# Second half of the first weight slab issued by another engine, narrower dummies, and a split last store in a two-layer SiLU kernel

## The chip, the cores and the metric

The kernel runs on one core of a Trainium2 chip. A core has five engines, each with its own instruction stream: TensorE (PE, matrix multiplications into PSUM), VectorE (DVE), ScalarE (ACT), GpSimd (POOL) and SyncE (SP). They wait for one another through semaphores. Data comes from and goes to the device memory by DMA: SyncE and ScalarE issue a transfer, which then runs by itself on 16 shared DMA engines and raises a semaphore when it has landed. The metric is the device time of one execution in microseconds (us), taken as the median of several runs.

## The reference

```python
# x: (1, 2048, 640), w1: (640, 1728), w2: (1728, 640), all bf16
h = jnp.einsum("bsd,df->bsf", x, w1)
h = jax.nn.silu(h)
out = jnp.einsum("bsf,fd->bsd", h, w2)
```

## The kernel before

The first layer is computed with the hidden dimension on the partitions: `hT` holds 13 tiles of 128 hidden columns, and a tail of 64 in `hTt`. The inner dimension of 640 is cut into five pieces k = 0 to 4 of 128. The 2048 rows of x are taken in four pieces c of 512. x must be there with its inner dimension on the partitions (`xT`), so it is loaded by transposing DMAs (`turned`, L119), three for each piece c: k = 0 and 1, k = 2 and 3, k = 4. The weights `w1s` of the first eight hidden tiles come as five slabs, one for each k (`load_k`, L125; 256 KB each); slab 0 comes in two halves of four hidden tiles (128 KB each). The other hidden columns follow in two loads (L165 to 169).

For the first piece c = 0 the order is by slabs: `k_pass(k)` (L201) runs eight matmuls, one for each hidden tile, into eight PSUM banks, and the five passes k add up there. Pass k = 0 needs the first x load and the first half of slab 0; ahead of its fifth matmul it waits for the second half (L203 and 204). After that come the remaining five hidden tiles of c = 0, then the pieces c = 1 to 3, then the tail. ScalarE takes each finished bank through Silu into `hT` (L195).

The second layer follows without a break on TensorE: for each of 16 tiles of 128 rows, `finish` (L297) adds 13 matmuls of 512 output columns to what `open_pair` began, and VectorE and ScalarE in turn copy the bank to `o_sb` (`evac`, L252). The last 128 of the 640 output columns are made separately, turned (`oT`), and put into `o_sb` by a transposing DMA before the last ten tiles are computed (L329 to 351). `store` (L310) lets SyncE wait for the evictions of a tile and write it to the output. The last tile is made in two parts, columns 0 to 384 and 384 to 512; the second part is stored together with the last 128 columns, so its store has 256 columns.

Some things stand before the start. The program begins with a preamble that ends in a barrier of all engines. `ahead_of_start` (L98) puts an instruction before an engine's part in this barrier, and `barrier_wait_here` (L109) moves an engine's wait for it to the place where it is called. Ahead of the barrier SyncE issues the first x load, slab 1, the second x load, slab 2 and slab 3 (L156 to 162); ScalarE issues the first half of slab 0. VectorE clears a tile `z`, and TensorE runs 14 dummy matmuls of 256 columns on it (L141 to 148), whose results nobody reads; the fourth one raises a semaphore. ScalarE waits for that (L172), issues the second half of slab 0 (L173), and only then waits for the barrier (L174). TensorE waits for the barrier after pass k = 1 (L214), SyncE after all its weight loads (L170). After the barrier GpSimd clears `warm`, and ScalarE runs one Silu on it, which loads the table of that function (L176 to 178).

Of the kernel before, what the change touches and what calls it, by code (L numbers as in the profile page):

```python
# [9 lines left out]
def bass_standalone__dense_activation_silu__prompt_kernel(  # L10
# [6 lines left out]
    bf16 = mybir.dt.bfloat16  # L17
# [3 lines left out]
    of = out.flatten_outer_dims()  # L21
    S, D = xf.shape
    F = w1.shape[1]
    P = 128
    NB = 8
# [5 lines left out]
    HB = 256  # L31
    NSC = S // SCH
    DA = 512
# [4 lines left out]
    pe, act, dve, pool, sp = nc.tensor, nc.scalar, nc.vector, nc.gpsimd, nc.sync  # L38

    with ExitStack() as es:  # L40
        def sb(name, shape, dtype):
            return es.enter_context(nc.sbuf_tensor(name, shape, dtype))

        xT = sb("xT", [P, DT, S], bf16)
        w1s = sb("w1s", [P, DT, F], bf16)
# [4 lines left out]
        oT = sb("oT", [P, S], bf16)  # L50
        o_sb = sb("o_sb", [P, S // P, D], bf16)
        warm = sb("warm", [P, 32], fp32)
        z = sb("z", [P, HB], bf16)
        ps = es.enter_context(nc.psum_tensor("ps", [P, NB, BANK], fp32))

        count = {}
# [2 lines left out]
        def sem(name):  # L59
            s = es.enter_context(nc.semaphore(name))  # L60
            count[s.name if hasattr(s, "name") else name] = 0
            return [s, 0]

        def tick(ins, s, n=1):
            ins.then_inc(s[0], n)
            s[1] += n
            return (s, s[1])

        def wait(eng, *points):
            for pt in points:  # L70
                if pt is None:
                    continue
                s, v = pt
                key = (id(eng), id(s))
                if seen.get(key, 0) < v:
                    eng.wait_ge(s[0], v)
                    seen[key] = v

        s_pe, s_act, s_dve = sem("s_pe"), sem("s_act"), sem("s_dve")
# [4 lines left out]
        def load(eng, out_ap, in_ap):  # L84
            s = sem(f"s_ld{n_dma[0]}")
            n_dma[0] += 1
            return tick(eng.dma_start(out=out_ap, in_=in_ap), s, 16)

        ET = mybir.EngineType

        def preamble(engine, opcode):
            lst = nc.main_func.blocks[0].instructions
            return next(
                i for i, ins in enumerate(lst)
                if ins.opcode == opcode and ins.engine == engine
            )

        def ahead_of_start(emit, engine):  # L98
            lst = nc.main_func.blocks[0].instructions
            n = len(lst)  # L100
            r = emit()
            lst = nc.main_func.blocks[0].instructions
            new = lst[n:]
            del lst[n:]
            at = preamble(engine, "Drain")
            lst[at:at] = new
            return r

        def barrier_wait_here(engine):  # L109
            lst = nc.main_func.blocks[0].instructions  # L110
            lst.append(lst.pop(preamble(engine, "EventSemaphore")))

        w1_v = w1.rearrange("(dt p) f -> p dt f", p=P)
        w2_v = w2[0:F0, :].rearrange("(ft p) d -> p ft d", p=P)

        FA = 8
# [8 lines left out]
        def load_k(eng, k):  # L125
            return load(eng, w1s[:, k, 0:FA * P], w1_v[:, k, 0:FA * P])
# [6 lines left out]
        def first(i):  # L133
            k0, k1 = KT[i]
            pt = turned(0, k0, k1, s_x[i])
            for k in range(k0, k1):
                ld_x[k] = pt
        p_z = ahead_of_start(lambda: tick(dve.memset(z[:, :], 0.0), s_dve), ET.DVE)  # L138
        bank_free = [None] * NB

        def dummies(n):  # L141
            for _ in range(n):
                ins = pe.matmul(ps[:, 3, 0:HB], lhsT=z[:, 0:P], rhs=z[:, :], start=True, stop=True)  # L143
            return tick(ins, s_pe)

        wait(pe, p_z)
        p_d0 = dummies(4)
        dummies(10)

        FH = FA // 2  # L150
        ld_k = {}

        def slab(k):
            ld_k[k] = load_k(sp, k)

        ahead_of_start(lambda: first(0), ET.SP)  # L156
        ld_k0a = ahead_of_start(
            lambda: load(act, w1s[:, 0, 0:FH * P], w1_v[:, 0, 0:FH * P]), ET.Activation)
        ahead_of_start(lambda: slab(1), ET.SP)
        ahead_of_start(lambda: first(1), ET.SP)  # L160
        ahead_of_start(lambda: slab(2), ET.SP)
# [3 lines left out]
        for a, b in FG:  # L165
            e = F if b == FT else b * P
# [1 line left out]
            for ft in range(a, b):  # L168
                ld_w1[ft] = pt
        barrier_wait_here(ET.SP)  # L170

        wait(act, p_d0)  # L172
        ld_k[0] = load(act, w1s[:, 0, FH * P:FA * P], w1_v[:, 0, FH * P:FA * P])  # L173
        barrier_wait_here(ET.Activation)  # L174

        p_warm = tick(pool.memset(warm[:, :], 0.0), s_pool)  # L176
        wait(act, p_warm)
# [3 lines left out]
        for c in range(1, NSC):  # L181
# [6 lines left out]
            load(sp, w2t[0:FL, :], w2[F0:F, :]),  # L188
            load(sp, w2t[FL:2 * FL, :], w2[F0:F, :]),
        ]  # L190

        def mm(o, l, r, start, stop, shared=False):
            return pe.matmul(o, lhsT=l, rhs=r, start=start, stop=stop, skip_group_check=shared)  # L193
# [30 lines left out]
        for ft in range(FA, FT):  # L224
            wait(pe, ld_w1[ft])
            b = bank()
            for k in range(DT):
                ins = mm(ps[:, b, :], w1s[:, k, ft * P:(ft + 1) * P], xT[:, k, 0:SCH],
                         start=(k == 0), stop=(k == DT - 1))
            silu(hT[:, ft, 0:SCH], ps[:, b, :], b, tick(ins, s_pe))  # L230
        for c in range(1, NSC):
            wait(pe, ld_xc[c])
            for ft in range(FT):
                b = bank()
                for k in range(DT):
                    ins = mm(ps[:, b, :], w1s[:, k, ft * P:(ft + 1) * P],
                             xT[:, k, c * SCH:(c + 1) * SCH], start=(k == 0), stop=(k == DT - 1))
                h_last = silu(hT[:, ft, c * SCH:(c + 1) * SCH], ps[:, b, :], b, tick(ins, s_pe))
        h_tail = []
        for q in range(NSC // 2):  # L240
            b = bank()
            for k in range(DT):
                for hh in range(2):
                    c = 2 * q + hh
                    ins = mm(ps[hh * FL:(hh + 1) * FL, b, :], w1s[:, k, F0:F],
                             xT[:, k, c * SCH:(c + 1) * SCH],
                             start=(k == 0), stop=(k == DT - 1), shared=True)
# [4 lines left out]
        def evac(out_ap, in_ap, b, after, eng=None):  # L252
            e = eng or (dve, act)[evac_n[0] % 2]
            evac_n[0] += 1
            wait(e, after)
            if e is dve:
                r = tick(dve.tensor_copy(out=out_ap, in_=in_ap), s_dve)  # L257
            else:
                r = tick(act.copy(out=out_ap, in_=in_ap), s_act)  # L259
            bank_free[b] = r  # L260
            return r

        st_w = [None] * NSC
# [25 lines left out]
        JB = SCH // P  # L289
# [4 lines left out]
        last_st = order[-1]  # L294
# [13 lines left out]
            return fin  # L308

        def store(st, fin):  # L310
            lo = 0
            for a, e, r in fin:
                hi = D if e == DA else e
                wait(sp, r, st_w[st // JB])
                stores.append(load(sp, of[st * P:(st + 1) * P, lo:hi], o_sb[:, st, lo:hi]))
                lo = hi

        def open_pairs(sts):
            for i in range(0, len(sts), 2):
# [2 lines left out]
        stores = []  # L322
# [7 lines left out]
        for c in range(NSC):  # L330
            b = bank()
            wbank.append(b)
            for ft in range(FT):
                mm(ps[:, b, :], w2s[:, ft, DA:D], hT[:, ft, c * SCH:(c + 1) * SCH],
                   start=(ft == 0), stop=False)
        wait(pe, *h_tail)
        for q in range(NSC // 2):
# [6 lines left out]
            for hh in range(2):  # L344
                c = 2 * q + hh
                r = evac(oT[:, c * SCH:(c + 1) * SCH], ps[:, wbank[c], :], wbank[c], tt[hh])
# [5 lines left out]
        for st, fin in early:  # L352
            store(st, fin)
        for bt in batches[1:]:
            open_pairs(bt)
            for st in bt:
                store(st, finish(st))
# [29 lines left out]
```

## Time and profile before

| what | value |
|---|---|
| median of 5 runs | 125.82 us (125.63 to 125.92) |
| profiled execution, its own time | 125.91 us |
| its span, from first to last instruction | 124.6 us |
| granted TensorE clock in it | 1.00 |
| TensorE busy | 121.1 us (97%), 588 matmuls |
| ScalarE busy | 38.1 us (31%) |
| VectorE busy | 7.5 us (6%) |
| DMA | 10.35 MB in 19285 packets |
| dummies | 14, mean 419 ns |
| first-layer matmuls | 280, mean 381 ns |

The span is shorter than the time, since the time also holds what lies before the first and after the last instruction. A matmul's duration reaches from its start to its modelled end; since matmuls are pipelined, the distance from one start to the next is shorter than the duration, and it is the distance that sets the time of a run of matmuls. A DMA row on SyncE or ScalarE gives the time that the engine spends on issuing; the landing comes later, and has a view of its own that gives the time from the start of the issue to the landing. The idle time printed behind an instruction names what released the engine.

### The profile page before, as it was taken

To read this page: it belongs to the slowest core of one execution; us is meant where nothing else is said; L and a number is where in the kernel's file an instruction comes from. 1 tells how busy PE (TensorE), PEld (TensorE's weight loads), DVE (VectorE), ACT (ScalarE), POOL (GpSimd) and SP (SyncE) were. 2 spreads that over 40 slices of the span, in tenths; PEclk is the share of its full clock that TensorE was granted. 3 is DMA by queue.
4 is the path that set the end of the run, shared out by engine and by line. 5 is a ranking of instruction groups with operands and counts; after the bars stand their busy time and mean duration, and the time that the engine had idled before them with its cause. 6 is when DMAs were issued, how large, how long until landed. Compare 5 with 4: busy or idle time off the path is not lost.

```text
span 124.6 us, 1342 instructions
## 1 busy us (share of the span) xinstructions
PE 121.1 (97%) x588; PEld 55.2 (44%) x588; DVE 7.5 (6%) x12; ACT 38.1 (31%) x66; POOL 0.3 (0%) x5
## 2 busy tenths in 40 slices
PE   8699999999999999999999999999999999999993
PEld 6144444444444444444434444444434444444452
DVE  0000000000000000000002020200012220102021
ACT  0400985555555555555530101010012101010100
POOL 0000000000000000000000000000000000000000
DMA  6999999799000000000000000000003377111112
GB/s 131 206 322 305 177 180 119 134 358 363 0 0 0 0 5 0 3 0 0 0 0 0 5 0 0 0 0 0 0 0 70 62 252 264 53 53 53 53 59 99
DMA packets 19285, 10.35 MB, mean 83 GB/s; under 512 B 13264, under 2 KB 18768, under 8 KB 19280
## 3 DMA queue, kind: packets, MB, share of 16 engines
q1 hardware_dynamic: 18992, 10.01, 31.7%
q10 hardware_dynamic: 288, 0.26, 0.9%
q8 instruction: 4, 0.07, 0.2%
q14 instruction: 1, 0.01, 0.0%
HBM read 4.51 MB, written 2.62 MB: 57 GB/s over the span
## 4 chain that ended last, share of the span: by engine, by line
PE 94%; DMA 4%; issue 0%; ACT 0%; DVEq 0%
PE ps L193 94%; DMA w1s<-in_w_dram 4%; PE ps L143 1%; ACT o_sb L259 0%; DVEq L372 0%
## 5 line engine op out<-in xcount | busy, mean ns | idle before, releaser
L193 PE MATMUL ps<-xT,w1s 128*128 128x512 bf16 (+1 forms) x280 | 59.1, 381 | 1.1 <-DMA w1s<-in_w_dram 1.1
L193 PE MATMUL ps<-w2s,hT 128*128 128x512 bf16 (+2 forms) x221 | 45.4, 367 | 0.0
L193 PEld LDWEIGHTS ps<-xT,w1s 128*128 128x128 bf16 (+1 forms) x280 | 26.4, 99 | 33.7 <-DMA w1s<-in_w_dram 1.6
L197 ACT ACTIVATE hT<-ps 128x512 bf16<-128x512 f32 x52 | 30.0, 608 | 25.8 <-PE ps L193 25.8
L193 PEld LDWEIGHTS ps<-w2s,hT 128*128 128x128 bf16 x221 | 20.9, 98 | 24.4 <-issue 1.1
L259 ACT CAST o_sb<-ps 128x512 bf16<-128x512 f32 (+1 forms) x8 | 4.4, 545 | 42.2 <-PE ps L193 42.2
L257 DVE CAST o_sb<-ps 128x512 bf16<-128x512 f32 (+1 forms) x9 | 6.1, 676 | 101.1 <-PE ps L193 101.1
L193 PE MATMUL ps<-hT,w2s 128*128 128x512 bf16 x52 | 11.4, 379 | 0.0
L193 PEld LDWEIGHTS ps<-hT,w2s 128*128 128x128 bf16 x52 | 5.1, 98 | 6.1
L259 ACT CAST oT<-ps 128x512 bf16<-128x512 f32 x2 | 1.1, 588 | 11.0 <-PE ps L193 11.0
L143 PE MATMUL ps<-z 128*128 128x256 bf16 x14 | 3.2, 419 | 0.4 <-DVE z L138 0.4
L178 ACT ACT_TABLE_LOAD x1 | 1.3, 1283 | 4.8 <-DVEq L372 4.8
L143 PEld LDWEIGHTS ps<-z 128*128 128x128 bf16 x14 | 2.0, 146 | 1.1 <-DVE z L138 0.4
L193 PE MATMUL ps<-w2t,hTt 64*128 64x512 bf16 (+2 forms) x17 | 2.2, 366 | 0.0
L257 DVE CAST oT<-ps 128x512 bf16<-128x512 f32 x2 | 1.3, 686 | 13.7 <-PE ps L193 13.7
L197 ACT ACTIVATE hTt<-ps 128x512 bf16<-128x512 f32 x2 | 1.2, 597 | 1.1 <-PE ps L193 1.1
L193 PEld LDWEIGHTS ps<-w2t,hTt 64*128 64x128 bf16 x17 | 0.7, 94 | 1.4 <-issue 0.8
L193 PE MATMUL ps<-hTt,w2t 64*128 64x512 bf16 x4 | 0.6, 382 | 0.0
L193 PEld LDWEIGHTS ps<-hTt,w2t 64*128 64x128 bf16 x4 | 0.1, 94 | 0.4 <-issue 0.4
L178 ACT ACTIVATE warm<-warm 128x32 f32<-128x32 f32 x1 | 0.2, 229 | 0.0
L138 DVE MEMSET z<- 128x128 uint32 x1 | 0.2, 165 | 0.2 <-issue 0.2
L176 POOL MEMSET warm<- 128x32 f32 x1 | 0.1, 124 | 4.3 <-POOLq L372 4.3
(4 smaller groups left out, 0.4 us busy)
## 6 DMA issues: line engine op xcount, KB each, us to landing
out_dram<-o_sb SPq DMA_DIRECT2D x15, 160.0 KB, 1.9
w2s<-in_w_dram SPq DMA_DIRECT2D x1, 1120.0 KB, 5.7
w1s<-in_w_dram SPq DMA_DIRECT2D x4, 256.0 KB, 4.4
w2s<-in_w_dram SPq DMA_DIRECT2D x1, 960.0 KB, 7.8
w1s<-in_w_dram SPq DMA_DIRECT2D x1, 480.0 KB, 5.1
w1s<-in_w_dram SPq DMA_DIRECT2D x1, 400.0 KB, 5.9
w1s<-in_w_dram ACTq DMA_DIRECT2D x2, 128.0 KB, 3.4
xT<-in_x_dram SPq DMA_TRANSPOSE x12, 4.5
```

What stands on the lines that cost most here:

```text
L138: p_z = ahead_of_start(lambda: tick(dve.memset(z[:, :], 0.0), s_dve), ET.DVE)
L143: ins = pe.matmul(ps[:, 3, 0:HB], lhsT=z[:, 0:P], rhs=z[:, :], start=True, stop=True)
L176: p_warm = tick(pool.memset(warm[:, :], 0.0), s_pool)
L178: act.activation(out=warm[:, :], in_=warm[:, :], func=ACT.Silu)
L193: return pe.matmul(o, lhsT=l, rhs=r, start=start, stop=stop, skip_group_check=shared)
L197: r = tick(act.activation(out=out_ap, in_=in_ap, func=ACT.Silu), s_act)
L257: r = tick(dve.tensor_copy(out=out_ap, in_=in_ap), s_dve)
L259: r = tick(act.copy(out=out_ap, in_=in_ap), s_act)
```

## The change

There are three edits. The second half of slab 0 is issued by SyncE, ahead of the barrier, between the first x load and slab 1; ScalarE's wait for the dummies, its issue and the moved barrier wait are gone, so ScalarE waits for the barrier where the preamble has it. The dummy tile `z` has 128 columns, of which a repeating access pattern reads each twice, so a dummy still streams 256 columns; there are 13, and none raises a semaphore. Their code stands further down in the program, but on TensorE they are still the first instructions. In `store`, the last 128 columns of the last tile are stored on their own, as soon as they are turned, before SyncE waits for the two other parts; the last store has 128 columns.

```diff
-        z = sb("z", [P, HB], bf16)
+        z = sb("z", [P, P], bf16)
...
-        bank_free = [None] * NB
-
-        def dummies(n):
-            for _ in range(n):
-                ins = pe.matmul(ps[:, 3, 0:HB], lhsT=z[:, 0:P], rhs=z[:, :], start=True, stop=True)
-            return tick(ins, s_pe)
-
-        wait(pe, p_z)
-        p_d0 = dummies(4)
-        dummies(10)
-
         FH = FA // 2
         ld_k = {}
...
         ahead_of_start(lambda: first(0), ET.SP)
         ld_k0a = ahead_of_start(
             lambda: load(act, w1s[:, 0, 0:FH * P], w1_v[:, 0, 0:FH * P]), ET.Activation)
+        ld_k[0] = ahead_of_start(
+            lambda: load(sp, w1s[:, 0, FH * P:FA * P], w1_v[:, 0, FH * P:FA * P]), ET.SP)
         ahead_of_start(lambda: slab(1), ET.SP)
         ahead_of_start(lambda: first(1), ET.SP)
         ahead_of_start(lambda: slab(2), ET.SP)
...
         barrier_wait_here(ET.SP)
 
-        wait(act, p_d0)
-        ld_k[0] = load(act, w1s[:, 0, FH * P:FA * P], w1_v[:, 0, FH * P:FA * P])
-        barrier_wait_here(ET.Activation)
-
         p_warm = tick(pool.memset(warm[:, :], 0.0), s_pool)
...
+        bank_free = [None] * NB
+
+        z2 = z[:, :].rearrange("p (o n) -> p o n", o=1).to_broadcast([P, HB // P, P])
+
+        def dummies(n):
+            for _ in range(n):
+                pe.matmul(ps[:, 3, 0:HB], lhsT=z[:, 0:P], rhs=z2, start=True, stop=True)
+
+        wait(pe, p_z)
+        dummies(13)
...
         def store(st, fin):
-            lo = 0
+            def out_cols(a, e):
+                stores.append(load(sp, of[st * P:(st + 1) * P, a:e], o_sb[:, st, a:e]))
+
+            wait(sp, st_w[st // JB])
+            if st == last_st:
+                out_cols(DA, D)
             for a, e, r in fin:
-                hi = D if e == DA else e
-                wait(sp, r, st_w[st // JB])
-                stores.append(load(sp, of[st * P:(st + 1) * P, lo:hi], o_sb[:, st, lo:hi]))
-                lo = hi
+                wait(sp, r)
+                out_cols(a, D if st != last_st else e)
```

## The prediction

> **What bounds the kernel now.** I read the page's busy shares first: TensorE (PE) is busy 97% of a span of 124.6 us, so only what delays the first long run of matmuls, interrupts it, or follows the last one can count. Then the chain of work that ended last, in order of time (start us, length us, what):
>
> ```profile
> 0.39 1.05 PE ps L143 x4
> 1.44 0.02 issue
> 1.46 4.48 DMA w1s<-in_w_dram
> 5.94 0.05 issue
> 5.99 116.67 PE ps L193 x569
> 122.66 0.02 issue
> 122.68 0.27 ACT o_sb L259
> ```
>
> The reader is to see three pieces: a weight load that ScalarE issues at 1.46, after four dummies, and that lands at 5.94; then 569 matmuls without a gap from 5.99 on; then the last eviction, and its store up to 124.6. So whatever moves the start of the unbroken run moves the end one for one, unless a later load is not there in time. The timeline of the first 12 us shows what stands before that start (start us, length us, engine, line, idle before it):
>
> ```profile
> 0.39 3.17 PE L143 MATMUL ps<-z 128*128 128x256 bf16 x14 [0.39 <-DVE z L138]
> ...
> 3.52 1.35 PE L193 MATMUL ps<-xT,w1s 128*128 128x512 bf16 x4
> ...
> 5.99 6.22 PE L193 MATMUL ps<-xT,w1s 128*128 128x512 bf16 x28 [1.12 <-DMA w1s<-in_w_dram]
> ```
>
> Four matmuls of pass k=0 run on the first half of weight slab 0, then TensorE stands still for 1.12 us for the second half. The issue view, taken for a window that holds just these two issues (KB, us from issue to landing), gives the two loads that decide:
>
> ```profile
> w1s<-in_w_dram SPq DMA_DIRECT2D x1, 256.0 KB, 4.8
> w1s<-in_w_dram ACTq DMA_DIRECT2D x1, 128.0 KB, 4.5
> ```
>
> The second half of slab 0 lands at 1.46 + 4.5 = 5.96, slab 1 at 1.39 + 4.8 = 6.2: both are in flight together. Slab 1 isn't waited for now, since its pass begins at 5.99 + 4 x 0.216 = 6.85. SyncE's issues ahead of the barrier:
>
> ```profile
> 0.00 1.33 SPq L120 DMA_TRANSPOSE xT<-in_x_dram  x1
> 1.39 0.56 SPq L87 DMA_DIRECT2D w1s<-in_w_dram  x1
> 2.01 1.24 SPq L120 DMA_TRANSPOSE xT<-in_x_dram  x1
> 3.29 1.05 SPq L87 DMA_DIRECT2D w1s<-in_w_dram  x2
> ```
>
> **Rates.** 28 matmuls in 6.22 us, less the 0.38 that the last one takes, are 0.216 us each (512 columns). Fourteen dummies in 3.17, less 0.42, are 0.2115 each for 256 columns, so 0.423 for 512: half the rate. The first four real ones take (1.35 - 0.38) / 3 = 0.323 from start to start, 0.32 us more than at full rate, so about 1.5 of them ran at half rate: the rate rises near 3.52 + 1.5 x 0.423 = 4.15, which is 3.8 us after the first dummy. The row's granted clock is 1.00 throughout and doesn't show this; the spacing does.
>
> **The change, part by part.**
>
> 1. *Second half of slab 0 from SyncE, behind the first transposed load.* Its issue moves from 1.46 (ScalarE, behind the wait for four dummies) to 1.39, where slab 1's issue stands now. In a queue of its own order it is then behind the first x load, which lands at 3.52, and ahead of slab 1. Bounds for its landing: 1.39 + 2.4 = 3.8 (the first half took 2.4 us) and 1.39 + 4.5 = 5.9 (as now). TensorE is ready for it at 3.52 + 0.97 + 0.216 = 4.71 and done with it, if it is there, at 4.71 + 4 x 0.216 = 5.57. Then it wants slab 1. Any landing up to about 5.5 therefore has the same answer, and I take one in that part of the range.
>
> 2. *What is late next: slab 1.* Every issue behind the moved one on SyncE's queue moves by one issue. ScalarE's rows for this same piece are 0.34 and 0.38 us long, SyncE's for the larger slab 0.56; with the 0.06 between issues that is 0.40 to 0.62; I take 0.42, the row of the same shape. Slab 1's landing: 6.2 if it is set by the bytes that share the DMA engines (the same 384 KB as now, in another order), 6.2 + 0.42 to 6.2 + 0.62 if it rides on its issue. I take half of the shift, 6.4, because both loads start well after issue now and land within 0.3 us of each other, which speaks for sharing, while nothing excludes that the issue counts. Pass k=1 then starts at 6.4 + 0.05 (the issue gap of the chain) = 6.45 in place of 6.85: **0.40 us gained** of the 1.12.
>
> 3. *The later passes.* k=2 starts at 6.45 + 8 x 0.216 = 8.18. With 0.42 added in full, its x load (2.01 + 5.1 = 7.1) comes at 7.5 and slab 2 (3.29 + 4.4 = 7.7) at 8.1: just in time. k=3 at 9.91 has slab 3 at 8.8, k=4 at 11.6 slab 4 at 10.4, the next weight columns 11.9 against 13.4, the last 13.2 against 16.6, and the next 512 rows of x (third load 12.57 + 4.3 = 16.9) 17.3 against 18.8. No new wait, if nothing slips by more than the 0.42; the tightest cover is 0.1 us, at slab 2.
>
> 4. *Barrier.* SyncE reaches it after its early issues, so it also opens some 0.42 later. Behind it stand the POOL memset and ScalarE's table load (4.75, 1.28 us) and warm activation (to 6.28). ScalarE's next work, the first Silu, comes after 6.2 us more of waiting for TensorE: the shift is hidden, and would cost only past that. TensorE's own barrier wait was moved behind pass k=1 already and is met after 5.57, when the barrier has been open. SyncE's wait stands behind loads that have 1 us and more of cover in step 3. ScalarE's removed wait for the dummies had nothing behind it that decides.
>
> 5. *Dummies.* One fewer: TensorE is free 0.21 us earlier, and still waits for x at 3.52. The memset of half the width saves between nothing and half of 0.165 us, hidden the same way. Reading 128 columns twice has no row: taken at nothing, the same 256 columns per dummy. Thirteen could take 3.13 / 13 = 0.24 each before they touch 3.52, and a further 0.4 us would vanish in the wait for slab 1 up to there. The tick on the fourth dummy is nothing. What the missing dummy can do to the rate is a rival below.
>
> 6. *The last stores.* The new store of 32 KB is issued after 120.56 + 0.33 = 120.9 while SyncE waits for the next eviction until 122.54: hidden, and landed by 122.6 at 1.6 us. The final store shrinks from 64 to 32 KB. Isolated stores take 1.7 (160 KB), 1.6 (96 KB), 1.6 us (64 KB): nothing to 0.1 us gained, and as rows of 256 B have no store in this trace, up to 0.1 lost. I take **0.05 gained**. One more semaphore to wait for at the end lies ahead of the last landing (hidden).
>
> [...]
>
> **Sum.** 0.40 + 0.05 = 0.45. The profiled execution took 125.91 us (span 124.6 and 1.3 around it): 125.91 - 0.45 = 125.46. The median of the runs, 125.82, lies 0.09 below it, so the forecast is 125.37.
>
> **Rivals.**
> - *B, more gain.* Slab 1 isn't delayed, or comes earlier because the second half no longer interleaves with it. The limit is then slab 2 at 7.7: k=2 at 7.75 in place of 8.58, 0.83 gained, with the store 124.94. For it: the DMA share is high (1.04 at 3.5 to 4.9 us), so bytes rather than issues may rule.
> - *C, the wait stays.* Behind the transposed load the half slab lands 4.5 us after its issue as now, 5.89: 0.07 + 0.05 gained, 125.70. For it: the only difference is the queue. Against: slab 1 shared the engines with it.
> - *D, slower: slab 1 becomes the wait.* In one queue slab 1 pays both the later issue (0.62) and the 128 KB ahead of it (0.13 MB at the 304 GB/s of the stretch 4 to 5 us, 0.43): 6.2 + 1.05 = 7.25, pass k=1 at 7.30 in place of 6.85, 0.45 lost, 126.2 with the store. It decides from a landing of 6.80 on. Against: those 128 KB are moved in the same stretch now.
> - *E, the rate rises late.* Thirteen dummies end at 3.14 or up to 0.08 sooner, so TensorE is idle 0.38 to 0.46 us before the first matmul; now 0.17. If that restarts the 3.8 us count, the rise comes at 7.32: eight matmuls at 0.423 end at 6.90, one more at half rate, seven at 0.216, k=2 at 8.83 in place of 8.58: 0.25 lost, 126.02. Against: the 1.12 us gap at 4.87 doesn't lower the rate.
>
> [...]
>
> **Chances.** Forecast 0.42 (125.15 to 125.57), B 0.20, C 0.12, D 0.17, E 0.06, else 0.03. A difference of 0.2% (0.25 us) is about what the measurement can tell from none. Faster: forecast and B, 0.62. Same: C and half of E with its neighbours, 0.16. Slower: the rest, 0.22. The range runs from B's 124.9 to D's 126.2; beyond lie the ends of B, D and the unlisted.
>
> **What the new profile would show.** Right: the wait for w1s after the fourth matmul gone or under 0.3 us, a new one after the eighth until about 6.4, the half slab landing before 5.5, SyncE's issues behind it later by about 0.42, and a last store of 32 KB landing in at most 1.6 us. Wrong: slab 1 past 6.8 (D), the first eight matmuls all 0.42 us apart (E), the half slab at 5.9 (C), a wait ahead of k=2 (step 3), dummies further apart than 0.24 us (step 5).

## The result and the profile after

The median after is 125.46 us of 35 runs, against 125.68 us for the kernel before over 59 runs; the ratio is 0.9977 with a 95% interval of 0.9969 to 0.9986, so the change takes away 0.29 us (0.18 to 0.39); the means differ by as much, the medians by 0.22. The profiled execution took 125.61 us with a span of 124.2, against 125.91 and 124.6. Two kernels below scatter so widely that the comparison leaves some of their executions out: the one with the early half on ScalarE (all twelve times lie between 125.03 and 127.89) and the one with the second x load ahead of slab 1, whose profile is of such an execution (128.79 us; the five others took 126.53 to 127.27).

The chain of work that ended last, in the profile after (start us, length us, what), its latter part:

```profile
2.48 1.24 SPq L120
3.72 0.04 issue
3.77 4.40 DMA w1s<-in_w_dram
8.16 0.14 issue
8.30 114.06 PE ps L191 x557
```

The unbroken run now begins at 8.30 with 557 matmuls, where before it began at 5.99 with 569: twelve matmuls (four of pass k=0, eight of k=1) come ahead of the last wait. The load in the chain is another one. It was issued at 3.77, so it is slab 2. The timeline shows the same from TensorE's side:

```profile
1.41 1.03 SPq L87 DMA_DIRECT2D w1s<-in_w_dram  x2
2.48 1.24 SPq L120 DMA_TRANSPOSE xT<-in_x_dram  x1
3.44 3.80 PE L191 MATMUL ps<-xT,w1s 128*128 128x512 bf16 x16
...
8.30 4.04 PE L191 MATMUL ps<-xT,w1s 128*128 128x512 bf16 x18 [1.06 <-DMA w1s<-in_w_dram]
```

Sixteen matmuls, the passes k=0 and k=1, run almost without a stop; then TensorE stands still for 1.06 us. The stop of 1.12 us has moved on by twelve matmuls, and is about as long as it was. The issue view, in three windows that hold one issue each (1.41, 2.02 and 3.77: the half slab, slab 1, slab 2):

```profile
w1s<-in_w_dram SPq DMA_DIRECT2D x1, 128.0 KB, 3.0
...
w1s<-in_w_dram SPq DMA_DIRECT2D x1, 256.0 KB, 3.2
...
w1s<-in_w_dram SPq DMA_DIRECT2D x1, 256.0 KB, 4.4
```

The half slab is there at 4.43 (5.94 before), slab 1 at 5.2 (6.2), slab 2 at 8.16 (7.72). Pass k=2 starts at 8.30 in place of 8.59: 0.29 us in this pair of profiles. Behind it nothing has changed but the last store: from the start of pass k=2 to the end of the span are 116.00 us in the profile before, 115.91 after.

The changed kernel was profiled once more (e0 below). Slab 2 landed at 7.87 there, and pass k=2 again waited for it, but for 0.19 us only: slab 2 came 0.29 us sooner, and the sixteen matmuls ahead took 4.33 us in place of 3.80, since they ran longer at half rate, 0.43 us apart to about 4.9 us, where the profile above has full rate from 3.7 on (timeline):

```profile
3.48 4.33 PE L191 MATMUL ps<-xT,w1s 128*128 128x512 bf16 x16 [0.16 <-DMA xT<-in_x_dram]
8.00 4.26 PE L191 MATMUL ps<-xT,w1s 128*128 128x512 bf16 x19 [0.19 <-DMA w1s<-in_w_dram]
```

So the length of the stop isn't what the stop costs; what counts is the start of pass k=2.

### The profile page after: what moved, and what is told of

Read it like the earlier page. It is cut to its first block, busy times and chain, and to the rows that moved or that the text cites. A ratio compares the mean times of both kernels' runs of the same rounds, so it can differ in the third digit from the quotient of the medians.

```text
span 124.2 us, 1341 instructions
## 1 busy us (share of the span) xinstructions
PE 120.8 (97%) x587; PEld 54.9 (44%) x587; DVE 7.5 (6%) x12; ACT 38.1 (31%) x66; POOL 0.3 (0%) x5
## 2 busy tenths in 40 slices
DMA packets 19429, 10.35 MB, mean 83 GB/s; under 512 B 13536, under 2 KB 18912, under 8 KB 19424
## 4 chain that ended last, share of the span: by engine, by line
PE 92%; DMA 4%; SPq 3%; issue 0%; ACT 0%
PE ps L191 92%; DMA w1s<-in_w_dram 4%; SPq L120 2%; SPq L87 1%; ACT o_sb L257 0%
## 5 line engine op out<-in xcount | busy, mean ns | idle before, releaser
L191 PE MATMUL ps<-hT,w2s 128*128 128x512 bf16 x52 | 11.4, 379 | 0.0
```

## The experiments

The 116.00 and 115.91 us from the start of pass k=2 to the end of the span are of use for all that follows. In the profiles of before and of the two experiments with the old store this part is 116.00 us, and in those of all kernels with the new store 115.91 to 115.92. So a span less that constant gives the start of pass k=2 in executions whose trace isn't shown. The table has its mean over the runs of the comparison, beside that of before on the same chip. The ratio is the comparison's own and not the quotient of two means: for e1 the means differ by 0.39 us where the ratio makes 0.26, with both inside its interval.

| kernel | ratio to before (95%) | k=2 starts, mean us | before, same chip |
|---|---|---|---|
| e1, edit 1 alone | 0.9979 (0.9962 to 0.9996) | 7.80 | 8.19 |
| e2, store alone | 1.0002 (0.9988 to 1.0016) | 8.23 | 8.19 |
| e3, dummies alone | 1.0009 (0.9993 to 1.0025) | 8.24 | 8.19 |
| e5, one more small issue | 1.0004 (0.9992 to 1.0016) | 8.17 | 8.19 |
| e4, slab 2 by ScalarE | 0.9964 (0.9946 to 0.9982) | 7.93 | 8.39 |
| e6, half by ScalarE, early | 1.0026 (0.9985 to 1.0066) | 8.8 | 8.39 |
| e7, slab 2 ahead of x | 0.9954 (0.9937 to 0.9970) | 7.86 | 8.39 |
| e8, six dummies | 1.0052 (1.0025 to 1.0078) | 9.09 | 8.39 |
| e0, changed kernel again | 0.9972 (0.9957 to 0.9987) | 8.12 | 8.43 |
| e9, as e7 | 0.9953 (0.9938 to 0.9967) | 7.89 | 8.43 |
| e10, as e7, 15 dummies | 0.9961 (0.9947 to 0.9975) | 7.94 | 8.43 |
| e11, x ahead of slab 1 | 1.0097 (1.0078 to 1.0117) | 9.65 | 8.43 |

**Theories.** *Theory 1:* the wait moved from the half slab to slab 2, which lands about 4.4 us after its issue, and the issue is later by the half slab's. *Theory 2:* slab 2 is late for the bytes ahead of it in SyncE's queue. *Theory 3:* the dummies and the store bring the gain.

**Edit 1 alone (e1),** on the kernel before:

```diff
+        ld_k[0] = ahead_of_start(
+            lambda: load(sp, w1s[:, 0, FH * P:FA * P], w1_v[:, 0, FH * P:FA * P]), ET.SP)
         ahead_of_start(lambda: slab(1), ET.SP)
...
-        wait(act, p_d0)
-        ld_k[0] = load(act, w1s[:, 0, FH * P:FA * P], w1_v[:, 0, FH * P:FA * P])
-        barrier_wait_here(ET.Activation)
```

> Kernel before with the first edit alone: SyncE issues the second half of slab 0, fourteen dummies on the full tile, old stores. Theory 1 (the gain is the wait moved from the half slab to slab 2, whose landing rides on its issue at about 4.4 us): pass k=2 starts near 8.2 to 8.3 us in place of 8.58, so 0.3 us less than before, ratio near 0.9977. Theory 3 (the dummies and the store bring the gain): ratio near 1.000.

The ratio is 0.9979: this edit brings as much as the whole change. Its profile, too, has the passes k=0 and k=1 without a stop, and more than that (timeline):

```profile
3.35 8.97 PE L191 MATMUL ps<-xT,w1s 128*128 128x512 bf16 x38
```

There is no stop ahead of pass k=2 either, since slab 2 landed 3.5 us after its issue here, at 7.28, with the same loads in the same order (issue view, window of that issue):

```profile
w1s<-in_w_dram SPq DMA_DIRECT2D x1, 256.0 KB, 3.5
```

So the landing of slab 2 scatters from one execution to the next, and the 4.4 of theory 1 is no constant: over the profiles of kernels with slab 2 behind the second x load on SyncE's queue it is 3.5 to 4.8.

**Store alone (e2) and dummies alone (e3),** on the kernel before; e2 takes the new `store`, e3 this:

```diff
-        z = sb("z", [P, HB], bf16)
+        z = sb("z", [P, P], bf16)
...
-        dummies(10)
+        dummies(9)
```

with `rhs=z2`, the view that reads each column twice.

> Kernel before with the store edit alone. Theory 1: the last store of 32 KB lands 0.08 us sooner after its issue, ratio 0.9994, not to be told from 1. Theory 3 (dummies and store bring the gain): 0.2 us or more, ratio 0.998 or less.

> Kernel before with the dummy edit alone: half tile read twice, 4 + 9 dummies, the tick on the fourth stays and ScalarE still waits for it. Theory 1: within 0.1 us of before, all hidden by the 1.1 us wait for the half slab; the dummies stay 0.213 us apart. Theory 3: 0.2 us or more faster. If the rate rose late for want of one dummy, the first four matmuls would be 0.42 us apart, and still hidden by the wait up to 5.9.

Neither can be told from before, and theory 3 falls. The profile of e2 has the last store's row (issue view, window of that issue), 1.49 us from the trace's own numbers against 1.57 before:

```profile
out_dram<-o_sb SPq DMA_DIRECT2D x1, 32.0 KB, 1.5
```

That is the 0.08 us by which 116.00 became 115.91. In e3 the thirteen dummies take 2.95 us, 0.21 us from start to start, as before. The wait for the half slab hid whatever the rate did.

One cost of the dummy edit stands in no span. The time of an execution less its span is 1.32 to 1.34 us on the mean in the kernels with the full dummy tile (before on the three chips, e1, e2), 1.40 in e3, where before has 1.32 on the same chip, and 1.38 to 1.41 in all others with the half tile. So this edit costs 0.08 us outside the span (e3; 0.05 to 0.09 in the others), about what the store wins inside it, and what is left of the change is the earlier start. The number of dummies isn't the reason, since it is 1.40 with six (e8) and 1.41 with fifteen (e10); whether the narrow tile or the repeated read is, no run shows.

**One more issue (e5),** on the changed kernel:

```diff
+        ahead_of_start(lambda: load(sp, pad[:, :], w1_v[:, 0, 0:2]), ET.SP)
         ahead_of_start(lambda: slab(1), ET.SP)
```

> Kernel after with one more load on SyncE between the half slab and slab 1: 128 rows of 4 bytes into a tile that nobody reads, so an issue with next to no bytes. Theory 1 (slab 2 rides on its issue): SyncE's issues behind it move by 0.4 us, slab 2 lands 0.4 later at about 8.6, pass k=2 starts at 8.7, the kernel takes 0.4 us more than after, 0.1 more than before (ratio to before 1.000 to 1.002). Theory 2 (slab 2 is late for the bytes ahead of it in SyncE's queue, 128 KB more than before): no change from after, ratio to before 0.9977.

Slab 2's issue moved by 0.46 us with half a KB more in the queue. The ratio is 1.0004, and its interval lies above that of the changed kernel (0.9969 to 0.9986): the gain is gone. Against e1 on the same chip pass k=2 starts 0.37 us later. So bytes are not the cause, and theory 2 falls; on the mean what is queued ahead of slab 2 counts, as theory 1 has it. The added load also has 144 packets of its own (19573 in the whole execution against 19429), as many as a half slab has, so this run doesn't part the issue from the packets. In the single profile it doesn't show, because slab 2 took 3.8 us there (issue view, then timeline):

```profile
w1s<-in_w_dram SPq DMA_DIRECT2D x1, 256.0 KB, 3.8
```

```profile
8.21 4.04 PE L193 MATMUL ps<-xT,w1s 128*128 128x512 bf16 x18 [0.54 <-DMA w1s<-in_w_dram]
```

**Slab 2 by ScalarE (e4),** on the changed kernel, after nine of the dummies, and **the half slab by ScalarE (e6),** at once:

```diff
-        ahead_of_start(lambda: slab(2), ET.SP)
...
+        wait(act, p_d)
+        ld_k[2] = load_k(act, 2)
+        barrier_wait_here(ET.Activation)
```

```diff
-            lambda: load(sp, w1s[:, 0, FH * P:FA * P], w1_v[:, 0, FH * P:FA * P]), ET.SP)
+            lambda: load(act, w1s[:, 0, FH * P:FA * P], w1_v[:, 0, FH * P:FA * P]), ET.Activation)
```

> Kernel after, with slab 2 issued by ScalarE behind a wait for the ninth dummy (about 2.4 us) in place of SyncE at 3.77. Theory 1 (rides on the issue): slab 2 lands at 2.4 + 4.4 = 6.8 us, the wait of 1.06 us ahead of pass k=2 goes, and only what slab 1 loses to interleaving stays; up to 1 us less than after, ratio to before 0.990 to 0.995. Theory 2 (bytes): slab 2 and slab 1 share the engines, slab 1 becomes late by what slab 2 gains, ratio 0.997 or more.

> Kernel after, with the second half of slab 0 issued by ScalarE right behind the first half, with no wait for dummies; SyncE's issues are as early as in before. Theory 1: slab 2 issued at 3.3 lands at 7.7, the half slab by 4.5, so pass k=2 starts at 7.75: 0.5 us less than after, ratio to before 0.993 to 0.994, unless the first x load comes later than 3.4 for the 128 KB beside it, which costs as much as it is late. Theory 2 (bytes): slab 2 comes no earlier than in after, ratio 0.997 to 0.998.

In e4 slab 2 landed at 6.53 and is waited for no more; but the half slab beside it came at 5.09 and the second x load at 7.54 (6.26 after). The timeline has the stop back in its old place, shorter:

```profile
5.14 7.08 PE L197 MATMUL ps<-xT,w1s 128*128 128x512 bf16 x32 [0.44 <-DMA w1s<-in_w_dram]
```

Less than theory 1 allowed was won (0.9964, an interval that overlaps that of the changed kernel): what slab 2 won on ScalarE's queue, the loads beside it on SyncE's queue lost. In e6 it is the first x load that loses, on which everything waits; it landed at 4.48 in place of 3.4 (timeline):

```profile
4.53 7.68 PE L191 MATMUL ps<-xT,w1s 128*128 128x512 bf16 x28 [1.20 <-DMA xT<-in_x_dram]
```

The times of e6 have a median of 127.16 and scatter over nearly 3 us; its ratio decides nothing. Over all twelve, pass k=2 starts at 9.7 on the mean. The reservation in its expectation was the outcome in this profile.

**Slab 2 ahead of the second x load (e7, again as e9), and the contrary (e11).** By then a third form of the theory stood, *S:* a plain load queued right behind a transposing one lands 0.6 to 2.0 us after it, differently each time, and slab 2 stands there in the changed kernel (in its profile the x load landed at 6.26, slab 2 at 8.16).

```diff
-        ahead_of_start(lambda: first(1), ET.SP)
         ahead_of_start(lambda: slab(2), ET.SP)
+        ahead_of_start(lambda: first(1), ET.SP)
```

e11 instead puts `first(1)` ahead of `slab(1)`.

> Kernel after, with slab 2 issued ahead of the second x load on SyncE. Theory 1: slab 2 issued at 2.5 lands by 6.9, the second x load issued at 3.1 lands by 3.1 + 3.8 to 5.1 = 6.9 to 8.2; pass k=2 starts between 7.08 and 8.3, so 0 to 1.2 us less than after, ratio to before 0.988 to 0.998. Theory 2 (bytes): the last of the two lands when the same bytes have been moved, at 8.2, no change from after.

> Slab 2 ahead of the second x load, a second time, on one chip with the changed kernel. Theory S (a plain load queued right behind a transposing one lands 0.6 to 2.0 us after it, differently in each execution, and slab 2 in the changed kernel stands there): with slab 2 ahead, no wait before pass k=2 is left, 0.2 to 0.3 us less than the changed kernel, ratio to before 0.995 to 0.996. Theory 2 (bytes): equal to the changed kernel, 0.9977.

> Changed kernel with the second x load issued ahead of slab 1, so that slabs 1 and 2 both stand behind a transposing load. Theory S: that load lands near 5.6, slab 1 0.6 to 2.0 us behind it at 6.2 to 7.6, pass k=1 starts there in place of 5.35; slab 2 0.7 later; pass k=2 at 8.0 to 9.3: 0 to 0.7 us more than the changed kernel. Theory 2 (bytes): slab 1 lands when the same bytes have moved as now for the second x load, 6.3, slab 2 at 8.2 as now, no change from the changed kernel.

In e7 the stop ahead of pass k=2 is gone (timeline):

```profile
3.47 8.76 PE L191 MATMUL ps<-xT,w1s 128*128 128x512 bf16 x36
```

Slab 2 landed at 6.3 and the x load at 7.5, before 7.75, when TensorE came to it (issue view, windows of the issues at 2.48 and 2.96):

```profile
w1s<-in_w_dram SPq DMA_DIRECT2D x1, 256.0 KB, 3.8
...
xT<-in_x_dram SPq DMA_TRANSPOSE x1, 4.5
```

Theory 2 had 8.2. Slab 3, now the load behind the x load, landed 0.54 us after it, a little under the bounds of S. Beside the changed kernel on one chip, pass k=2 starts 0.23 us earlier on the mean (7.89 against 8.12), as S expected; the intervals of the two ratios overlap, so of the two versions this is the likelier, not the proven best. Against before it is 0.46% faster, twice. e11 costs 1.0% instead, more than S allowed: slab 1 landed 2.2 us after the x load ahead of it, at 8.06 (timeline, then the stretches: us, PE busy, other engines, granted clock, DMA share, GB/s):

```profile
3.61 2.37 PE L191 MATMUL ps<-xT,w1s 128*128 128x512 bf16 x8 [0.29 <-DMA xT<-in_x_dram]
8.11 4.17 PE L191 MATMUL ps<-xT,w1s 128*128 128x512 bf16 x11 [2.13 <-DMA w1s<-in_w_dram]
```

```profile
8.10:11.40 3.30, 3.29 (x8) 1.16 (x9) 0.00 (x0) 0.00 (x0) 0.00 (x0) 0.50 0.89 232
11.50:16.00 4.50, 4.45 (x22) 2.02 (x22) 0.00 (x0) 0.67 (x2) 0.00 (x0) 1.00 1.11 236
```

After the long stop the clock was granted at half, and pass k=1 took 3.3 us. The other five executions, with a clock of 1.00, still have k=2 at 9.2 to 9.9, more than a microsecond later than the changed kernel's 8.12 without that fall; that slab 1 is late in them too is likely, but they have no trace.

**Six dummies (e8) and fifteen (e10).** e8 has `dummies(6)` in the changed kernel, e10 `dummies(15)` in that of e7.

> Kernel after with 6 dummies in place of 13, so TensorE is idle from 1.6 to 3.4 us. If dummies are needed for the rate to rise: the first eight matmuls and some of pass k=1 run 0.42 us apart; up to 7.2 us or so hidden by the wait for slab 2 at 8.2, so 0 to 0.5 us more than after. If the rate needs no more than these: no change from after.

> Slab 2 ahead of the second x load, and 15 dummies in place of 13, which end at 3.57 instead of 3.15, so that TensorE isn't idle before its first matmul. Theory R (the moment at which the rate rises depends on when the execution starts, not on the small gap): equal to the kernel with 13, within 0.15 us. Rival E of the prediction (the gap holds the rate back): up to 0.7 us less and a narrower spread.

The timelines of e8 and of e10:

```profile
0.38 1.46 PE L185 MATMUL ps<-z 128*128 128x256 bf16 x6 [0.38 <-DVE z L138]
3.60 8.73 PE L191 MATMUL ps<-xT,w1s 128*128 128x512 bf16 x32 [1.76 <-DMA xT<-in_x_dram]
```

```profile
0.37 3.38 PE L185 MATMUL ps<-z 128*128 128x256 bf16 x15 [0.37 <-DVE z L138]
3.54 8.83 PE L191 MATMUL ps<-xT,w1s 128*128 128x512 bf16 x34
```

In e10, 34 matmuls take (8.83 - 0.38) - 33 x 0.216 = 1.32 us more than at full rate. Each microsecond at half rate (their weight loads stand 0.43 us apart, in place of 0.216) loses half, so they ran at half rate for some 2.65 us, to 6.2. The same sum gives 6.9 for e8 and 3.8 for the changed kernel. By the distances between matmuls it is 3.7 for the changed kernel (0.33 us from the first to the second, 0.216 behind them). In the profiles with thirteen to fifteen dummies, and no long stop behind them, the rate rose at moments from 3.7 to 6.2 us; e10 and e9 can't be told apart (0.9961 and 0.9953), and the spans of e10 spread no less. So filling the small gap ahead of the first matmul bought nothing, and rival E found no support. Six dummies were too few: 0.5% slower than before. Pass k=2 starts 0.70 us later than in before on that chip, where the changed kernel starts 0.31 earlier than before on its own: about 1 us more, twice the most that the expectation allowed. The profile, with 8.71, is in the better half of the executions; by their spans the others reach 9.8.

## Why the prediction was right or wrong, point by point

The sign and the range held, and 125.37 is near 125.46; but the gain, which is what was forecast, is 0.29 us in place of 0.45, and it is limited at another place than the prediction had it. That the time came so near is in part luck: the forecast was taken off a median of 125.82 from five runs, and the median of 59 is 125.68. The wait ahead of k=2 was one of the prediction's own signs of being wrong, and the wait after the eighth matmul, one of its signs of being right, didn't come.

- *Step 1, the half slab:* right. It landed at 4.43, inside the bounds and before 5.5, and its wait is gone; e1 shows that this edit is the gain.
- *Step 2, slab 1:* wrong. The prediction said "Slab 1's landing: 6.2 if it is set by the bytes that share the DMA engines", later if it rides on its issue, and took 6.4. It landed at 5.19 after, at 5.2 to 5.4 in the other profiles with these loads in this order: a microsecond sooner, outside both bounds. Part of the microsecond is scatter, since e2 and e3, with the old order, have slab 1 at 5.7. Issued from two queues, the two loads both ended late (half slab 5.4 to 5.9, slab 1 5.7 to 6.2, in before, e2 and e3); in one queue the half slab is through at 4.4 to 4.7 and slab 1 follows. Taking the old landing as a floor was the mistake: an order was treated as if only its sum of bytes counted. The stated reason for rival B, that the half slab "no longer interleaves with it", fits this; the landings show what came of the other queue, and no run takes the interleaving apart from the rest.
- *Step 3, the later passes:* the landing was right and its consequence wrong. Slab 2 was put at 8.1, "just in time" for a pass at 8.18, and landed at 8.16. With slab 1 early, TensorE came to it at 7.1 and waited 1.06 us. The term of the sum that failed is therefore the 0.40: it was the way to slab 1's landing, and what it should have held is the way from the old start of pass k=2 to slab 2's landing, 8.59 less 8.30 = 0.29 (0.31 on the mean of e0's chip). That 0.40 came out near is luck: a slab 1 at 6.4 and a slab 2 at 8.1 happen to put the start of k=2 at about the same 8.18. The forecast had both slabs late, rival B had slab 1 early and left slab 2 at its old 7.7; the profile has slab 1 early and slab 2 late. e5 shows the other half: one more load ahead of slab 2 takes the gain back.
- *Scatter:* not foreseen. Slab 2 came 3.5 to 4.8 us after its issue, so single profiles of this start differ by up to a microsecond, and no forecast from one of them is good to 0.1 us.
- *Steps 4 and 5, barrier and dummies:* right inside the span, while the 0.08 us that the dummy edit costs outside it was put at nothing. The table load starts at 5.22 (4.75 before), and ScalarE still waits 5.4 us for its first Silu. The memset takes 0.11 us for 0.165, the dummies stay 0.21 us apart, and the ratio of e3 can't be told from 1.
- *Step 6, the stores:* 0.08 gained for a forecast of 0.05. The "up to 0.1 lost" for rows of 256 B was the author's estimate, with no row of before behind it. These rows landed no later, in 1.49 us against 1.57 for rows of 512 B and twice the bytes: a loss by the shorter rows, if there is one, is less than the halved bytes save. In the time the 0.08 is taken back outside the span.
- *Rival C* is excluded by the landing at 4.43, *D* by slab 1 at 5.19. *E* found no support in e10.

## What to carry to other kernels

A wait that is removed is worth only the distance to the next late load (0.29 us here, of a wait of 1.12): list the landings of all loads behind it, shift each by the issues that the change puts ahead of it, and pair the early case of one with the shifted case of the next. A second queue need not help: the half slab came sooner in order on one queue with slab 1 (4.1 to 5.0 in the profiles with nothing beside it) than from the other queue beside slab 1 (5.4 to 5.9 in before, e2 and e3). Where loads that transpose and plain loads share a queue, try the plain load that is needed first ahead of the transposing one; here that is likely worth 0.23 us, and slab 1 behind it cost 1.5 (e11). Compare such starts by many runs, not by one profile, and look at the time outside the span too.

## What the runs showed of the hardware

A 256 KB load with the same place in the queue, slab 2 behind the second x load, landed between 3.5 and 4.8 us after its issue; of the 256 KB loads right behind the second x load, the distance to that load's landing was 0.5 us (slab 3 in e7) to 2.2 (slab 1 in e11). Why some executions take longer stays open.

TensorE's rate rose at a moment that differs by 2.5 us between executions (3.7 to 6.2, with thirteen to fifteen dummies from 0.38 on; 7.5 in e6, which stood still for 1.2 us behind them), and only the distances between matmuls show it: the granted clock reads 1.00 all that time. What sets the moment, no run shows.

In e11's profile the rate fell back after a stop of 2.13 us, and the granted clock reads 0.50 from 8.1 to 11.4 us, while the stops of 1.1 us in before and after left it at full, with 0.216 us from matmul to matmul behind them. That is one execution, and no profile has a stop of a length in between at full rate.
